# Edits to the schedule of a two-layer convolution and MLP kernel: when transforms, stores, inverses, products and statistics are issued

## The chip, the cores and the metric

The kernel runs on one core of a Trainium2 chip. A core has a matrix engine (TensorE, "PE" in the profile), a vector engine (VectorE, "DVE"), an activation engine (ScalarE, "ACT"), a general one (GpSimd, "POOL") and SyncE ("SP"), which here issues every transfer. Each engine runs its own queue in order and waits on semaphores. The metric is device time in microseconds (us), the median of several executions: 2731.35 us before (2731.3 to 2731.46, three runs).

## The reference: what is computed

Two layers, each an operator A and then an operator B, on 2048 tokens of 1024 channels, all in float32:

```python
def A(x, k, v, shift_k, ssm_k, ssm_D):
    k_shift = causal_conv4(k, shift_k)              # four taps per channel
    kv = k_shift * v
    y = irfft(rfft(kv, 2 * S) * rfft(ssm_k, 2 * S))[:S]   # long causal conv per channel
    return x * (y + kv * ssm_D)

def B(x, w1, b1, w2, b2):
    return relu(x @ w1 + b1) ** 2 @ w2 + b2         # 1024 -> 3584 -> 1024

x = q
x = x + A(layernorm(x), k, v, shift_k, ssm_k, ssm_D)
x = x + B(layernorm(x), w1, b1, w2, b2)
x = x + A(layernorm(x), k, v, shift_k, ssm_k, ssm_D)
x = x + B(layernorm(x), w1, b1, w2, b2)
```

Both layers use the same k, v and filter, so the convolution's result y is computed once and read twice.

## The kernel before, in words

**Units.** The tokens are cut into four blocks of 512. The matrix work is eight units, one for a layer and a block, in the order (layer, block) = (0,0), (1,0), (0,1), (0,2), (1,1), (0,3), (1,2), (1,3). A unit is a row of steps; a step is one piece of weights, mostly 12 matmuls of 512 columns ("the main stream"). A float32 product is made of three matmuls on operands split into a high and a low part (`mm3`, lines 335 to 337). The split of a weight costs a copy on ScalarE (line 1012) and a subtraction on VectorE, at some steps on GpSimd (line 1020); some weights are stored split and loaded back (`wd_m`, line 1010). Between the first and the second unit the block is the same, so the second begins without a break: the last 28 steps of the first unit and the first of the second are made for half the tokens each (6 matmuls a step, later 12 of 256 columns), and the layer norm of each half (`chain`, line 1632) runs meanwhile. The last three units use a scheme with fewer products (`WINO`).

**Convolution.** It runs beside the units, for blocks 1 to 3 (the first block is done ahead of the first unit). Two streams, ticked `FWD_RATE` times a step, transform the inputs channel group by channel group (eight groups of 128 a block):

- `fwd_x` (line 353): loads k and v, four taps and the product with v on VectorE (lines 365 and 367), after some ticks the transposes on TensorE (line 420), the transform (391), sums on VectorE (402 to 407), stores to `xd` (412).
- `fwd_g` (line 429): loads the filter and a carried spectrum `kd`, the transform on TensorE (454), the copy of the new spectrum (459), its store for the next block (463), VectorE's sums (464 to 484), stores to `gd` (493). The PSUM banks `pt` of both streams are taken with `hold` and freed with `give`.

For the second block (`sb <= PLAIN`) the transforms are single float32 matmuls, for the later ones `mm3`. `const_split` splits the transform tables once, when the third block begins.

`prod_stream` multiplies the spectra: GpSimd's product (line 525), two ticks later VectorE's reduction (529), after three products of a group the fold and the butterfly on GpSimd (675 to 680), then the inverse on TensorE (595 for the second block), a copy and a store. Its rate is `pace`: the work of some blocks over the steps left for them, less `PACE_SLACK`. It holds what it is owed; a call gives one product at least, or a None when data is missing, and then the forward streams get one tick more.

**Statistics.** In all units but the first, `prep_a` loads the next block's rows into one of two `px` buffers and takes their mean and variance, from step 28. The bias of a unit is loaded into the same two buffers (line 1737) and added by GpSimd (1741, or 1599 in the last three units).

**Queues.** SyncE issues all transfers in program order, weights among them. A store that waits for its data holds back what is behind it.

Of the kernel before, what the change touches and what calls it, by code (L numbers as in the profile page):

```python
# [21 lines left out]
NT = T // P  # L22
NB = S // T
KT = D // P
FT = F // P
FC = 7
NCH = FT // FC
BL = 256
# [16 lines left out]
AHEAD_0 = 4  # L45
BURST = 1.06
FIN = "GGG"
PACE_SLACK = {1: 74, 3: 10}
PACE_TO = {1: 2}
PLAIN = 1  # L50
FILL = (16, 12, 8)
# [14 lines left out]
PIECES = ((0, 0), (0, 1), (1, 0), (1, 1))  # L66
WLO = {"b": "GGGV", "x": "GGGV"}
PREP_PACE = 0.2
FWD_RATE = {0: 1.4, 1: 1.4, 2: 1.4, 3: 1.1, 4: 1.1, 5: 1}


# [169 lines left out]
def tile_h3_mlp(ctx: ExitStack, tc: tile.TileContext, q, kT, vT, shk, ssmT, ssmD, w1, b1, w2, b2,  # L241
# [111 lines left out]
    def fwd_x(sb, c):  # L353
        k4 = mkfx([P, T + 3])
        SY.dma_start(k4, kT[c * P:(c + 1) * P, sb * T:sb * T + T + 3])
        v4 = mkfx([P, T])
        SY.dma_start(v4, vT[c * P:(c + 1) * P, sb * T:(sb + 1) * T])
        for _ in range(FWD_WAIT):
            yield
        ks = mkfx([P, T])  # L360
        w = shkt[:, c]
        A.activation(ks, k4[:, 3:], AF.Copy, scale=w[:, 0:1])
        yield
        for s in range(1, 4):
            V.scalar_tensor_tensor(ks, k4[:, 3 - s:T + 3 - s], w[:, s:s + 1], ks, op0=OP.mult, op1=OP.add)
        yield
        V.tensor_mul(ks, ks, v4)
        for _ in range(4 if sb == 1 else 7):
            yield
        o, = yield from hold(1)  # L370
        transposes(o, ks)
        yield
        if sb <= PLAIN:
            xt = mkfx([P, T])
            A.copy(xt, o)
        else:
            hi = mkfx([P, T], F32R)
            lo = mkfx([P, T], F32R)
            A.copy(hi, o)
            yield  # L380
            V.tensor_sub(lo, o, hi.bitcast(F32))
        yield
        give(o)
        yield
        oa = yield from hold(2)
        for e in range(2):
            for r in range(2):
                q_ = slice(e * 256, e * 256 + 256)
                ou = oa[e][:, r * 256:r * 256 + 256]
                if sb <= PLAIN:  # L390
                    PE.matmul(ou, plain[0][:, 2 * e + r], xt[:, q_], start=True, stop=True)  # L391
                else:
                    mm3(ou, fh[:, 2 * e + r], fl[:, 2 * e + r], hi[:, q_], lo[:, q_], True, True)
        yield
        odd = mkfx([P, T])
        A.copy(odd, oa[1])
        yield
        xo = cv.tile([P, 2, T], F32, name="fy", bufs=1)
        xv = xo.rearrange("p r (n u c) -> p u (r n) c", u=2, c=CG)
        ev = oa[0].rearrange("p (n c) -> p n c", c=CG)  # L400
        ov = odd.rearrange("p (n c) -> p n c", c=CG)
        V.tensor_add(xv[:, 0], ev, ov)
        V.tensor_sub(xv[:, 1], ev, ov)
        yield
        give(*oa)
        x2 = mkfx([P, T])
        V.tensor_add(x2, xo[:, 0], xo[:, 1])
        yield
        yield
        for i in range(3):  # L410
            t = x2 if i == 2 else xo[:, i]
            SY.dma_start(dview(XD[i], sb, c), t.rearrange("p (g b u) -> p g b u", g=2, b=BT))
        yield
# [15 lines left out]
    def fwd_g(sb, c):  # L429
# [28 lines left out]
        for r in range(2):  # L458
            A.copy(kk[r][:, BL:], oa[r])
        yield  # L460
        if sb < NB - 1:
            for r in range(2):
                SY.dma_start(KD[sb][c][:, r], kk[r][:, BT * BL:])
        V.scalar_tensor_tensor(kk[1][:, 0:T], kk[1][:, 0:T], sgn[:, 1:2], oa[0], op0=OP.mult, op1=OP.add)
        V.scalar_tensor_tensor(oa[1], kk[0][:, 0:T], sgn[:, 0:1], oa[1], op0=OP.mult, op1=OP.add)
        yield
# [20 lines left out]
            yield  # L487
            yield
        give(*oa)
        yield  # L490
        yield
        for i in range(3):
            SY.dma_start(dview(GD[i], sb, c), go[i].rearrange("p (g b u) -> p g b u", g=2, b=BT))
        yield
# [4 lines left out]

    def fwd_stream(kind, fwd):  # L500
        for sb in range(1, NB):
            if sb > PLAIN:
                const_split()
            for c in range(KT):
                yield from fwd(sb, c)
                half_done[kind].add((sb, c))
                if all((sb, c) in d for d in half_done.values()):
                    plag.at(3, fwd_done.add, (sb, c))

    streams = [fwd_stream("x", fwd_x), fwd_stream("g", fwd_g)]  # L510

    def fwd_tick():
# [6 lines left out]
    def prod_stream():  # L519
# [11 lines left out]
        def fin(st, sm, sb, g, k):  # L531
# [4 lines left out]
                lag.at(1, fin, st, sm, sb, g, 1)  # L536
            elif k == 1 and sb <= PLAIN:
                st["z"] = butterfly(E, s)
                lag.at(2, fin_plain, st, sb, g, 0)
            elif k == 1:  # L540
                pair = st["pair"]
                if "l" not in pair if g % 2 else inv[1] < inv[0]:
# [1235 lines left out]
    for s, (k, u, c, a, i, tts, w) in enumerate(steps):  # L1778
# [3 lines left out]
        if u != cur_u:  # L1782
            cur_u = u
            if u:
                xT = nxt
            bst = {}
            if u in WINO:
                wacc, rp = {}, {}
# [99 lines left out]
            early.append(load_y(b, HALF[0]))  # L1888
        if u + 1 < NU and not direct[u]:
            n = s - start_step[u]  # L1890
            if n == 28:
                pa = prep_a(*ORDER[u + 1])
            elif n > 28 and pa is not None and next(pa, 0) == 0:
                pa = None
            if u in WINO and left == W_PREP:
                nxt = prep_w(*ORDER[u + 1], lag)
            elif u not in WINO and left == 18:
                while pa is not None:
                    if next(pa, 0) == 0:
                        pa = None  # L1900
                close_conv(ORDER[u + 1][1])
                nxt = prep_b(*ORDER[u + 1], lag)
# [6 lines left out]
                next(tgen[0], None)  # L1909
        busy = left <= 18 and u + 1 < NU  # L1910
        rate = pace.get(u, 100) * (PREP_PACE if busy else 1.0)
        if len(tts) < NT:
            rate *= 0.1
        owed += rate
        todo = min(owed, BURST * rate)
# [64 lines left out]
```

## Time and profile before

| what | value |
|---|---|
| median of three runs | 2731.35 us |
| the profiled execution | 2731.19 us |
| its span in the trace | 2729.4 us |
| TensorE busy | 2683.3 us (98%) |
| VectorE busy | 1989.7 us (73%) |
| GpSimd busy | 843.9 us (31%) |
| DMA, mean | 277 GB/s |

The trace is of one execution. Busy times are shares of the span; a matmul's end is modelled, so TensorE's pace is read from the starts of matmuls that follow each other. "Idle before" names the time for which an engine stood ahead of an instruction, and what released it. The main stream's matmuls are counted from the end of the first block's own part; the first unit's half steps begin at 1272 and the second unit's full steps at 1632.

### The profile page before, as it was taken

The page shows a single profiled execution, that of the slowest core. Times are in us where ns is not written, and L with a number is a line of the kernel's source. Part 1 is how long each engine was busy: PE and PEld are TensorE (multiplying, and loading weights), DVE is VectorE, ACT ScalarE, POOL GpSimd, SP SyncE. Part 2 cuts the span into 40 slices and gives each one's busy share as a digit, 9 for nine tenths or more (in the row PEclk, how much of TensorE's full clock was granted, in tenths as well). Part 3 has the DMA queues.
Part 4 walks back from the last instruction along what each step waited for, and adds up shares of the span by engine and source line. Part 5 has one row for each costly group of instructions (what it writes and reads, how often), then busy time and mean ns, then how long its engine had stood idle before and what let it go on. Part 6 is the DMA issues. An engine that isn't in the chain of part 4 may idle for free.

```text
span 2729.4 us, 36532 instructions
## 1 busy us (share of the span) xinstructions
PE 2683.3 (98%) x12568; PEld 2228.9 (82%) x12568; DVE 1989.7 (73%) x3066; ACT 1124.2 (41%) x1936; POOL 843.9 (31%) x532
## 2 busy tenths in 40 slices
PE   7999999999999999999999999999999999999999
PEld 6888787888888888888888888888788788888887
DVE  7878888788987877779677665366787666664555
ACT  4454344433444233442234422244455444445443
POOL 2336565345532655236543454000100010001000
PEclk9999999999999999999999999999999999999999
DMA  8789898699989898888977887688888866676545
GB/s 253 262 301 316 285 312 285 221 312 369 324 298 324 295 338 280 267 332 284 349 263 269 301 295 253 226 288 311 300 284 295 281 229 211 229 276 200 178 166 204
DMA packets 377482, 755.05 MB, mean 277 GB/s; under 512 B 43840, under 2 KB 159184, under 8 KB 377296
## 3 DMA queue, kind: packets, MB, share of 16 engines
q1 hardware_dynamic: 377296, 752.72, 80.6%
q8 instruction: 99, 1.62, 0.2%
q14 instruction: 87, 0.71, 0.1%
HBM read 602.63 MB, written 149.95 MB: 276 GB/s over the span
## 4 chain that ended last, share of the span: by engine, by line
PE 84%; DVE 6%; DMA 5%; issue 1%; POOL 1%; ACT 1%; SPq 1%; DVEq 0%; ACTq 0%; POOLq 0%
PE p L336 26%; PE p L335 26%; PE p L337 26%; DMA wr<-w 2%; PE p L1095 2%; DVE whl L1020 1%; PE pt L335 1%; PE pt L337 1%; PE pt L336 1%; DMA whl<-wd_m 1%; DVE sm L529 0%; DMA cx<-xd 0%; PE pt L391 0%; DMA cg<-gd 0%; PE p L789 0%
## 5 line engine op out<-in xcount | busy, mean ns | idle before, releaser
L525 POOL TENSOR_TENSOR cp<-cx,cg 128x384 f32<-128x384 f32 (+5 forms) x288 | 541.8, 1893 | 580.3 <-DVE sm L529 388.1
L335 PE MATMUL p<-xh,whl 128*128 128x512 f32 (+1 forms) x1840 | 706.6, 384 | 3.3 <-DMA whl<-wd_m 2.5
L337 PE MATMUL p<-xh,whl 128*128 128x512 f32 (+1 forms) x1840 | 703.6, 382 | 3.6 <-DVE whl L1020 2.8
L336 PE MATMUL p<-xl,whl 128*128 128x512 f32 (+1 forms) x1840 | 702.8, 382 | 0.1
L1012 ACT CAST whl<-wr 128x512 fp32r<-128x512 f32 x637 | 383.5, 619 | 441.6 <-PE p L337 262.4
L1020 DVE TENSOR_TENSOR whl<-wr,whl 128x512 fp32r<-128x512 f32 x622 | 500.4, 825 | 78.4 <-ACT whl L1012 73.2
L335 PE MATMUL p<-whl,rh 128*128 128x512 f32 x1372 | 548.1, 399 | 3.7 <-ACT whl L1012 2.4
L336 PE MATMUL p<-whl,rh 128*128 128x512 f32 x1372 | 543.7, 396 | 1.9 <-POOL whl L1020 1.7
L337 PE MATMUL p<-whl,rl 128*128 128x512 f32 x1372 | 542.6, 396 | 0.0
L337 PEld LDWEIGHTS p<-xh,whl 128*128 128x128 f32 x1840 | 345.9, 188 | 71.7 <-DVE whl L1020 3.0
L335 PEld LDWEIGHTS p<-xh,whl 128*128 128x128 f32 x1840 | 346.2, 188 | 70.5 <-DMA whl<-wd_m 2.6
L336 PEld LDWEIGHTS p<-xl,whl 128*128 128x128 f32 x1840 | 346.0, 188 | 66.1 <-DVE xl L1408 0.3
L335 PEld LDWEIGHTS p<-whl,rh 128*128 128x128 f32 x1372 | 259.5, 189 | 64.0 <-ACT whl L1012 3.9
L336 PEld LDWEIGHTS p<-whl,rh 128*128 128x128 f32 x1372 | 259.5, 189 | 61.9 <-POOL whl L1020 2.6
L337 PEld LDWEIGHTS p<-whl,rl 128*128 128x128 f32 x1372 | 259.4, 189 | 60.6
L1502 DVE TENSOR_TENSOR rl<-wr,rh 128x512 fp32r<-128x512 f32 x140 | 141.1, 1009 | 182.8 <-ACT rh L1497 182.7
L1599 POOL TENSOR_TENSOR acc<-acc,px 128x512 f32<-128x512 f32 x18 | 23.1, 1317 | 771.0 <-DMA px<-b 771.0
L529 DVE TENSOR_REDUCE sm<-cp 128x128 f32<-128x384 f32 (+5 forms) x288 | 249.3, 874 | 9.2 <-POOL cp L525 9.2
L1494 ACT ACTIVATE wr<-p,b1t 128x512 f32<-128x512 f32 x138 | 95.2, 690 | 379.1 <-PE p L337 375.3
L1563 DVE TENSOR_TENSOR rl<-wr,rh 128x256 fp32r<-128x256 f32 x84 | 49.8, 593 | 208.5 <-ACT rh L1558 208.4
L1622 DVE TENSOR_TENSOR acc<-p,acc 128x512 f32<-128x512 f32 x152 | 101.5, 687 | 87.3 <-PE p L337 86.9
L1555 ACT ACTIVATE wr<-p,b1t 128x512 f32<-128x512 f32 x84 | 57.9, 689 | 190.4 <-PE p L337 188.9
(277 smaller groups left out, 3310.9 us busy)
## 6 DMA issues: line engine op xcount, KB each, us to landing
whl<-wd_m SPq DMA_DIRECT2D x379, 512.0 KB, 5.1
wr<-w SPq DMA_DIRECT2D x493, 256.0 KB, 5.4
wr<-td SPq DMA_DIRECT2D x152, 256.0 KB, 4.1
wd_m<-whl SPq DMA_DIRECT2D x70, 512.0 KB, 6.0
cx<-xd SPq DMA_DIRECT2D x48, 512.0 KB, 5.7
cg<-gd SPq DMA_DIRECT2D x48, 512.0 KB, 6.4
gd<-fg SPq DMA_DIRECT2D x72, 256.0 KB, 6.2
cx<-xd SPq DMA_DIRECT2D x48, 384.0 KB, 5.8
```

The source lines that it names most:

```text
L335: PE.matmul(o, lh, rh, start=start, stop=False)
L336: PE.matmul(o, lh, rl, start=False, stop=False)
L337: PE.matmul(o, ll, rh, start=False, stop=stop)
L525: G.tensor_mul(pr.rearrange("p c i -> p i c"), xt[:, 0:j + 1], gt[:, j::-1])
L529: V.tensor_reduce(sm[:, ty, jj], st["pr"], axis=AX.X, op=OP.add)
L1012: A.copy(t[:, 0], raws[n]["t"])
L1020: ENG[e[n % len(e)]].tensor_sub(t[:, 1], raws[n]["t"], t[:, 0].bitcast(F32))
L1095: PE.matmul(o, lh, r, start=start, stop=stop)
L1494: A.activation(r, st["o"], AF.Relu, bias=b1t[:, st["f"]:st["f"] + 1])
L1502: V.tensor_sub(st["lo"], st["r"]["t"], st["hi"].bitcast(F32))
L1555: A.activation(r, st["o"], AF.Relu, bias=b1t[:, st["f"]:st["f"] + 1])
L1622: V.tensor_add(accs[tt][:, d], o, accs[tt][:, d])
```

## The change

Line numbers in this text are those of the kernel before; the new file's differ by up to six, from line 510 to 1785 by four, so that 525 reads 529 and 1020 reads 1024.

- Second block, `fwd_x`: seven ticks instead of four between the product and the transposes.
- `fwd_g`: the carried spectrum is stored behind `give`, no longer ahead of the sums. Two ticks more ahead of the stores to `gd` for the second block.
- The third block's streams wait until the second unit has begun (`second`).
- Second block's inverse: three ticks behind the butterfly, not two.
- Statistics in the sixth and seventh unit from step 45, not 28.
- Products: `PACE_SLACK` 78 for 74; the rate falls to a tenth `QUIET` = 4 steps ahead of the half steps too.

```diff
-PACE_SLACK = {1: 74, 3: 10}
+PACE_SLACK = {1: 78, 3: 10}
...
+QUIET = 4
...
-        for _ in range(4 if sb == 1 else 7):
+        for _ in range(7):
             yield
         o, = yield from hold(1)
         transposes(o, ks)
...
-        if sb < NB - 1:
-            for r in range(2):
-                SY.dma_start(KD[sb][c][:, r], kk[r][:, BT * BL:])
         V.scalar_tensor_tensor(kk[1][:, 0:T], kk[1][:, 0:T], sgn[:, 1:2], oa[0], op0=OP.mult, op1=OP.add)
...
         give(*oa)
-        yield
-        yield
+        if sb < NB - 1:
+            for r in range(2):
+                SY.dma_start(KD[sb][c][:, r], kk[r][:, BT * BL:])
+        for _ in range(4 if sb <= PLAIN else 2):
+            yield
         for i in range(3):
             SY.dma_start(dview(GD[i], sb, c), go[i].rearrange("p (g b u) -> p g b u", g=2, b=BT))
...
         for sb in range(1, NB):
+            while sb > PLAIN and not second:
+                yield
             if sb > PLAIN:
                 const_split()
...
+    second = []
...
                 st["z"] = butterfly(E, s)
-                lag.at(2, fin_plain, st, sb, g, 0)
+                lag.at(3, fin_plain, st, sb, g, 0)
...
             if u:
                 xT = nxt
+                second.append(u)
...
             n = s - start_step[u]
-            if n == 28:
+            at = 45 if u in WINO else 28
+            if n == at:
                 pa = prep_a(*ORDER[u + 1])
-            elif n > 28 and pa is not None and next(pa, 0) == 0:
+            elif n > at and pa is not None and next(pa, 0) == 0:
                 pa = None
...
-        if len(tts) < NT:
+        if len(tts) < NT or direct[u] and left < 4 * FC + QUIET:
             rate *= 0.1
```

What the order of instructions shows of it, at three places. First, SyncE's queue at the fourth channel group of the second block (`kd_3` is its carried spectrum, `wd_m` stored weights, `wr` raw weights, `cx` and `cg` operands of the products, `gd` the filter's spectra). Before, and then of the change:

```order
L463 DMA kd_3_88<-fk 128x256 x2
L1001 DMA wr<-w 128x512
L1004 DMA wr<-w 128x512
L1028 DMA wd_m_1_5_0_2445<-whl 128x1024
L1004 DMA wr<-w 128x512 x5
L625 DMA cx<-xd_73 128x512
L625 DMA cg<-gd_74 128x512
L1004 DMA wr<-w 128x512
L1028 DMA wd_m_1_6_0_2523<-whl 128x1024
L493 DMA gd_74<-fg 128x2x256
```

```order
L490 DMA kd_3_88<-fk 128x256 x2
L1008 DMA wr<-w 128x512
L1032 DMA wd_m_1_0_2_2609<-whl 128x1024
L1008 DMA wr<-w 128x512 x2
L629 DMA cx<-xd_71 128x512
L629 DMA cg<-gd_75 128x512
L629 DMA cx<-xd_72 128x512
L629 DMA cg<-gd_76 128x512
L494 DMA gd_74<-fg 128x2x256
```

The carried spectrum's store has moved towards that of `gd`, and other loads stand between them. Second, SyncE's queue where the first unit's half steps begin, before and then of the change (`yd` is the convolution's result, `fg` the filter's load for the third block, `xd` the input's spectra):

```order
L1004 DMA wr<-w 128x512
L606 DMA yd_102<-wr 512x1x64
L625 DMA cx<-xd_73 128x512
L625 DMA cg<-gd_74 128x512
L625 DMA cx<-xd_71 128x512
L625 DMA cg<-gd_75 128x512
L427 DMA fg<-ssmT 128x2x128 x2
L436 DMA fk<-kd_1_86 128x256 x2
L606 DMA yd_102<-wr 512x1x64
L1028 DMA wd_m_3_0_0_4506<-whl 128x1024
L1004 DMA wr<-w 128x512 x3
```

```order
L1008 DMA wr<-w 128x512 x7
L413 DMA xd_71<-fy 128x2x256
L413 DMA xd_72<-fy 128x2x256
L413 DMA xd_73<-fx 128x2x256
L629 DMA cx<-xd_72 128x512
L629 DMA cg<-gd_76 128x512
L1032 DMA wd_m_3_0_0_4363<-whl 128x1024
L1008 DMA wr<-w 128x512 x4
L1032 DMA wd_m_3_0_2_4401<-whl 128x1024
L1008 DMA wr<-w 128x512
L629 DMA cx<-xd_73 128x512
L629 DMA cg<-gd_74 128x512
```

The third block's loads are gone, seven weight loads stand together, and operand loads of products follow within the half steps (four more stand behind the last row). Third, GpSimd's queue where the second unit begins, before and then of the change (line 1741, now 1745, adds the bias; 1020, now 1024, splits a weight; 525, now 529, is a product):

```order
L1020 TENSOR_TENSOR whl<-wr,whl 128x512
L1741 TENSOR_TENSOR acc<-acc,px 128x1024 x4
L1020 TENSOR_TENSOR whl<-wr,whl 128x512
L525 TENSOR_TENSOR cp<-cx,cg 128x4x128
L1020 TENSOR_TENSOR whl<-wr,whl 128x512
L525 TENSOR_TENSOR cp<-cx,cg 128x3x128
L525 TENSOR_TENSOR cp<-cx,cg 128x4x128
```

```order
L1024 TENSOR_TENSOR whl<-wr,whl 128x512 x8
L1745 TENSOR_TENSOR acc<-acc,px 128x1024 x4
L529 TENSOR_TENSOR cp<-cx,cg 128x3x128
L529 TENSOR_TENSOR cp<-cx,cg 128x4x128
L1024 TENSOR_TENSOR whl<-wr,whl 128x512
L529 TENSOR_TENSOR cp<-cx,cg 128x3x128
L529 TENSOR_TENSOR cp<-cx,cg 128x4x128
L529 TENSOR_TENSOR cp<-cx,cg 128x3x128
L529 TENSOR_TENSOR cp<-cx,cg 128x4x128
L1024 TENSOR_TENSOR whl<-wr,whl 128x512
```

Two products stand between the bias and the next weight split now, where there was none, and four ahead of the one after it.

## Rows read from the trace of the kernel before

**Rows 1.** The page's part 1: engine, busy us, share, instructions.

```profile
PE 2683.3 (98%) x12568; PEld 2228.9 (82%) x12568; DVE 1989.7 (73%) x3066; ACT 1124.2 (41%) x1936; POOL 843.9 (31%) x532
```

**Rows 2.** Waits of TensorE from 200 to 2729 us: in total, times, longest.

```profile
PE pt L420 <- DVE fx L367: 6.9, 3, 6.0
PE p L335 <- DMA whl<-wd_m: 3.6, 4, 2.2
PE p L337 <- DVE whl L1020: 2.8, 1, 2.8
PE p L335 <- ACT whl L1012: 2.4, 2, 1.9
PE pt L595 <- DVE fg L484: 2.0, 1, 2.0
```

**Rows 3.** Timeline of TensorE, 285 to 310: start, us, instruction, idle before.

```profile
293.35 0.39 PE L337 MATMUL p<-whl,rl 128*128 128x512 f32 x1
293.58 1.05 PE L595 MATMUL pt<-sm,yh 128*128 128x128 f32 x8
300.66 1.10 PE L420 MATMUL pt<-ident,fx 128*128 128x128 f32 x4 [6.03 <-DVE fx L367]
...
304.97 0.63 PE L337 MATMUL p<-whl,rl 128*128 128x512 f32 x1
305.40 0.63 PE L335 MATMUL p<-whl,rh 128*128 128x512 f32 x1
```

**Rows 4.** Windows: us, busy PE, PEld, DVE, ACT, POOL, clock, DMA share, GB/s.

```profile
460.00:480.00 20.00, 17.90 (x69) 13.90 (x69) 10.10 (x16) 6.62 (x11) 2.32 (x2) 0.91 1.00 362
...
520.00:540.00 20.00, 20.00 (x171) 20.00 (x171) 12.17 (x14) 11.34 (x19) 9.11 (x6) 1.00 0.45 157
...
620.00:640.00 20.00, 20.00 (x98) 16.87 (x97) 19.86 (x25) 9.99 (x17) 15.28 (x9) 1.00 1.00 321
```

**Rows 5.** Timeline of VectorE, 282 to 302.

```profile
292.29 3.68 DVE L365 SCALAR_TENSOR_TENSOR fx<-fx,shkt 128x512 f32<-128x512 f32 x3
...
299.84 0.68 DVE L367 TENSOR_TENSOR fx<-fx 128x512 f32<-128x512 f32 x1
```

**Rows 6.** Waits of SyncE, 250 to 302.

```profile
SPq L493 <- DVE fg L484: 9.9, 2, 5.5
```

**Rows 7.** Waits of SyncE, 440 to 470.

```profile
SPq L493 <- DVE fg L484: 8.8, 1, 8.8
```

**Rows 8.** Timeline of TensorE, 440 to 480.

```profile
465.83 0.49 PE L335 MATMUL p<-whl,rh 128*128 128x512 f32 x1 [1.87 <-ACT whl L1012]
466.55 0.76 PE L336 MATMUL p<-whl,rh 128*128 128x512 f32 x1 [0.23 <-DVE whl L1020]
...
469.67 0.57 PE L337 MATMUL p<-whl,rl 128*128 128x512 f32 x1
```

**Rows 9.** Timeline of VectorE, 476 to 548.

```profile
522.21 1.00 DVE L1701 TENSOR_SCALAR wr<-acc,mv,rs 128x512 f32<-128x512 f32 x2
...
539.94 5.70 DVE L1502 TENSOR_TENSOR rl<-wr,rh 128x512 fp32r<-128x512 f32 x2
```

**Rows 10.** Timeline of GpSimd, 495 to 548.

```profile
534.24 10.85 POOL L1741 TENSOR_TENSOR acc<-acc,px 128x1024 f32<-128x1024 f32 x4
545.05 1.71 POOL L1020 TENSOR_TENSOR whl<-wr,whl 128x512 fp32r<-128x512 f32 x1
```

**Rows 11.** Timeline of TensorE, 480 to 560: two stretches.

```profile
518.77 0.39 PE L337 MATMUL p<-xh,whl 128*128 128x256 f32 x1 [2.78 <-DVE whl L1020]
...
526.57 1.04 PE L1710 MATMUL p<-ident,wr 128*128 128x128 f32 x8
...
546.82 0.39 PE L337 MATMUL p<-xh,whl 128*128 128x256 f32 x1 [0.81 <-POOL whl L1020]
```

**Rows 12.** Groups of GpSimd by line and shape: busy us, mean ns, idle before.

```profile
L525 POOL TENSOR_TENSOR cp<-cx,cg 128x512 f32<-128x512 f32 x48 | 71.5, 1490 | 15.4 <-DVE sm L529 15.4
```

**Rows 13.** Waits of SyncE, 1895 to 1942.

```profile
SPq L725 <- POOL fk L1599: 8.9, 1, 8.9
```

## The prediction

> **What bounds the kernel now.** Read the page's first part first: TensorE is busy for 2683.3 of 2729.4 us [rows 1]. Nearly all of it is work that the change neither adds nor takes away, so what can move is the 46 us of idle time, and time at the lower clock. What the first block loses comes ahead of everything the diff touches. Second, what TensorE waits for behind 200 us: 6.9 us for the second block's transposes, which want VectorE's product of line 367 (6.0 in one piece), 2.0 for an inverse behind line 484, 2.4 and 2.8 for weights split late, 3.6 for stored weights of which 2.2 in one piece [rows 2]. Third, the timeline around the longest. TensorE stands from 294.6 to 300.66; then twelve matmuls follow each other 0.43 us apart instead of 0.23, the pitch just before (304.97 to 305.40 against 293.35 to 293.58) [rows 3]: the 1.2 GHz level in place of 2.4. Twelve times 0.2, with the slower transposes, is 2.3 us more. So this place costs 8.3.
>
> Why was the product late? VectorE was never idle ahead of it. Three shifted multiplies from 292.29 took 3.68 us, and only at 299.84, behind adds and weight splits, came line 367 with 0.68 [rows 5]; the product itself is short, VectorE was behind. SyncE's queue suffers from the same lag: the filter spectrum's store (line 493) waited for line 484 for 9.9 us in two pieces [rows 6], and again for 8.8 us [rows 7]. Every load behind it waits too, which is where the weight that is late at 465.83 comes from [rows 8]. One lag of VectorE thus makes the waits at 294, 446 and 465 us.
>
> **The change part by part.** Counting main-stream matmuls in the order of instructions (12 are one step, 12 x 0.23 = 2.76 us), the second block's transposes stood 12 to 36 behind line 367 and stand 36 to 48 behind it now; the late one had 24. That is 2.8 us more slack. The store of line 493 moves from 12 to 36 matmuls behind the last line-484 add to 36 to 48. The store of the carried spectrum moves from at most 12 behind its copy to 48 or 60; its reader comes a whole block later, so I cost that at nothing. A channel now takes 132 matmuls instead of 122 (180 to 1104 against 180 to 1032 for seven), so VectorE has 8% less to do per step: over the roughly 300 matmuls (69 us) ahead of the late transposes, at a VectorE near full, 5.5 us. Together 8.3 us against a wait of 6.0, so it goes, with its clock loss: -8.3. The two smaller waits of the kind go: -0.9. What is late next is a split weight or an inverse of the same size; I leave +0.6 for it, bounds 0 and 6.0.
>
> The third block's first spectrum, which ran ahead of 1248 matmuls, is out of the first unit; the inverse behind its line 484 loses that wait: -2.0 (bounds 0 and -2.0). At 465.83 and 466.55 the wait is 1.87 and 0.23, and eight matmuls to 469.67 stand at the lower pitch, 1.6 [rows 8]: 3.7 in all (the window's clock of 0.91 says 1.8 for the last part [rows 4]). With the store no longer blocking and seven weight loads issued ahead of the halves this goes as well: -3.7.
>
> Against that, **the pause does not empty this stretch**. The rate falls to a tenth, but a stream with work owed still gives one product per step, and its start is later now: five products fall into the first half-steps where one did, and six loads of product operands (256 KB each) stand together in SyncE's queue ahead of a weight. The last two need the buffer of the product just issued, so SyncE waits for GpSimd there. Bounds 0 and 3.7 (the wait that stood here); I take 1.0, near the lower end, since eight half-steps of 1.38 us lie between that weight's load and its use.
>
> In the last half's layer norm, the constants' split (768 columns, about 1.0 us at the rate of the 0.68 us row), and ahead of its last normalisation three line-365 multiplies, 2.0 us at 0.68 [rows 5], 3.7 beside GpSimd, are new on VectorE. What lies beside them: the second norm ended near 523.2 [rows 9] for transposes at 526.57 [rows 11], some 3 us of cover. The split is not covered, since the weight wait at 518.77 [rows 11] follows this chain; a reduce that leaves takes some of it back. I take +0.9, bounds 0 and 4.7 (all four, with the slow multiplies).
>
> **The start of the second unit** is where I expect the change to cost most. GpSimd adds the bias from 534.24 for 10.85 us; the weight split behind it started at 545.05 [rows 10] and TensorE waited 0.81 us for it [rows 11]. Now two products stand between, 1.49 us each [rows 12]: the split comes 3.0 us later. Two inverses moved ahead (0.9 more TensorE work by then) hide less than one; +3.0, bounds 0 and 8.3 (the longest wait with its clock).
>
> Beside these four adds two of VectorE's two-input operations of this width (0.68 us in [rows 5]) took 5.70 us [rows 9]. The Trainium skill, page "SBUF — State Buffer", section "Who interferes with whom", says that a VectorE instruction with two SBUF inputs and a GpSimd instruction that reads SBUF shut each other out for a whole instruction; the trace agrees with these rows, and by that rule the twelve products now issued between 1560 and 1680 matmuls speak against the change. What that would make of the time is the first rival.
>
> Second unit: the third block's products run from 1824 to 2304 matmuls for what had 1752 to 2280, 10% denser, and all its eight channels fall here. VectorE was already busy 19.86 of 20 us from 620 to 640, though TensorE kept its 20.00 there [rows 4]. +1.5, bounds 0 and 8.3. The pace constant (74 to 78) lies inside this: the products end at the same step.
>
> Statistics: in the sixth unit SyncE waited 8.9 us to load the next row block into a buffer that GpSimd's bias add held [rows 13], and stored weights came 2.2 us late, the longest of their four [rows 2]. The loads now stand behind the add, at step 45: -2.2. VectorE's own wait for the first row block stays as it was.
>
> Sum: -8.3 -0.9 -2.0 -3.7 -2.2 = -17.1; +0.6 +1.0 +0.9 +3.0 +1.5 = +7.0; together -10.1. The profiled execution took 2731.19 us (its span and 1.8 around it), 0.16 under the median of 2731.35; against the median, 2721.2.
>
> On the clock: 2.78 us of waiting at 518.77 [rows 11] was followed by the upper level (1.00 from 520 to 540), 1.87 at 465.83 by the lower (0.91 from 460 to 480) [rows 4]. The Trainium skill, page "TensorE: Matmul & The Clock Gate", section "Part 1: The HAM clock gate", says that idling brings the half rate and activity lifts it again; by that alone the new 3.8 us wait would cost about 2.3 more, 2723.5. Rows stand on both sides here, so the sum has none of it and the range has it.
>
> **Rivals.** (1) VectorE chained to GpSimd at the second unit's start. Each reduce there stands on VectorE ahead of a weight split and waits for a product that itself queues behind the 10.85 us of adds. For it: the rows above. Against it: weights are split three or more steps ahead, 8.3 us. Price: 3.0 becomes 8.3 with the clock, and another 1.5: 2728. (2) The pause doesn't do what it says, and the wait at the halves stays whole: 1.0 becomes 3.7, 2724. For it: five products and six loads in the order. Against: seven weights loaded first. (3) Slower: the lag only moves to the second unit. From 1824 matmuls on VectorE has more to do than the steps last; once it is more than the 8.3 us lead behind, each further us is TensorE's, and the store of line 493 there (12 to 36 matmuls behind its add, not moved for this block) blocks SyncE again, as it did twice in the first unit. Two such waits of 8.3 less the 1.5 already in the sum: 2721.2 + 15.1 = 2736.3, and with what stays of the first unit's, 2738. Against it: a full stretch there cost TensorE nothing before [rows 4], and 1680 to 1824 has fewer products than before.
>
> **How the numbers follow.** Chances: forecast 0.58, its own range 2714 to 2726; (1) 0.18, (2) 0.13, (3) 0.11. 0.2% is 5.5 us, about what a measurement of this kernel tells from no change: faster is under 2725.9, slower over 2736.8. Nearly all of the forecast and of (2) and a quarter of (1) are faster: 0.71; most of (1) and a third of (3) are the same: 0.21; the rest of (3) slower: 0.08. The range is 2713 (every gain, -17.1, and a little) to 2733, which leaves out most of (3).
>
> **What would show it.** Right: no wait of transposes for line 367 over 1 us and no clock under 1.00 around 300; SyncE's waits of line 493 under 4 us; no wait near 465; none for stored weights in the sixth unit; a wait of 3 to 4 us for GpSimd's split at the second unit's start. Wrong: a wait over 5 us anywhere from 440 to 720, a granted clock under 0.95 in the second unit, or a wait of the same size for line 367 at another channel.

## The result and the profile after

The changed kernel took 2742.34 us (median of six runs, 2738.1 to 2747.44) against 2731.32 us for the kernel before in runs beside it: ratio 1.0041, 95% interval 1.0027 to 1.0056. It is slower by 0.41%; the forecast was 2721.2 us with a range of 2713 to 2733. The profiled execution took 2740.9 us, its span is 2739.1 us, 9.7 more than before.

The page's first part: busy time and share of each engine. TensorE was busy for 2690.1 of 2739.1 us, so it idled 49.0 us in place of 46.1 [rows 1]; the mean granted clock fell from 0.998 to 0.996.

```profile
PE 2690.1 (98%) x12568; PEld 2231.4 (81%) x12568; DVE 1973.6 (72%) x3066; ACT 1123.1 (41%) x1936; POOL 841.0 (31%) x532
```

Waits of TensorE from 200 us to the end: what for, us in total, times, longest. They answer to [rows 2].

```profile
PE p L336 <- DMA whl<-wd_m: 6.9, 9, 2.0
PE p L336 <- ACT whl L1016: 5.3, 1, 5.3
PE p L338 <- DVE whl L1024: 3.3, 1, 3.3
PE pt L337 <- DVE yl L565: 2.4, 2, 1.7
PE pt L336 <- DVE fy L404: 2.4, 1, 2.4
PE p L338 <- POOL whl L1024: 1.7, 1, 1.7
```

The 6.9 us for line 367 are gone, whole, and so is the inverse's wait. In their place stand 5.3 us in one piece for a weight split, twice as much for stored weights, and sums and inverses of the third block that VectorE brings late. Where they lie is seen in windows (busy time of TensorE, weight loads, VectorE, ScalarE, GpSimd, then granted clock, DMA share, GB/s). The kernel before, four long stretches:

```profile
200.00:440.00 240.00, 233.15 (x1074) 193.97 (x1073) 209.22 (x298) 101.11 (x186) 147.99 (x119) 0.99 0.92 304
440.00:500.00 60.00, 53.50 (x232) 41.94 (x231) 47.99 (x87) 25.77 (x45) 20.18 (x15) 0.97 0.78 270
560.00:1000.00 440.00, 439.44 (x2074) 366.04 (x2073) 365.31 (x511) 171.00 (x308) 209.95 (x127) 1.00 0.94 326
1900.00:2720.00 820.00, 815.61 (x3571) 664.68 (x3571) 534.45 (x967) 384.23 (x632) 31.06 (x24) 1.00 0.71 240
```

The changed kernel, the same four, and three short ones in which the clock fell:

```profile
200.00:440.00 240.00, 240.00 (x1112) 199.82 (x1111) 203.86 (x295) 103.28 (x187) 142.81 (x116) 1.00 0.92 306
440.00:500.00 60.00, 53.73 (x267) 44.57 (x266) 47.31 (x91) 24.33 (x42) 16.51 (x13) 0.94 0.80 274
560.00:1000.00 440.00, 431.98 (x2031) 358.60 (x2030) 364.79 (x506) 170.31 (x307) 208.38 (x126) 1.00 0.93 324
1900.00:2720.00 820.00, 815.58 (x3562) 662.01 (x3560) 527.46 (x959) 385.64 (x636) 30.58 (x24) 1.00 0.70 237
...
460.00:480.00 20.00, 14.15 (x49) 10.70 (x48) 14.87 (x36) 5.57 (x10) 2.55 (x2) 0.83 0.62 220
500.00:520.00 20.00, 16.73 (x130) 16.53 (x129) 13.55 (x28) 7.68 (x14) 2.16 (x2) 0.91 0.32 118
740.00:760.00 20.00, 16.05 (x75) 13.29 (x74) 14.45 (x19) 6.39 (x12) 14.15 (x10) 0.91 0.91 309
```

From here on "loss" is TensorE's idle time plus, in 20 us windows, their length times what the granted clock lacks of 1 (idle time at a lower clock is in both). So counted, the change gave 10.5 us back from 200 to 440 us, and lost 1.4 more from 440 to 500, 3.9 from 500 to 540, 3.6 from 540 to 600, 8.5 from 600 to 1000 and 0.8 up to 1900; from 1900 on nothing moved (4.4 before and after). Together, with 0.3 won ahead of 200 us, a net loss of 7.4 of the 9.7 us; the rest is below what these windows resolve.

**The half steps.** Where the 5.3 us come from is read on three queues. On ScalarE the copy of the awaited weight (1016) stands behind the layer norm's activations (1685), and those wait for VectorE:

```profile
468.61 1.48 ACT L1685 ACTIVATE p<-acc,nm,rs 128x512 f32<-128x512 f32 x2 [1.28 <-DVE nm L1653]
471.50 1.49 ACT L1685 ACTIVATE p<-acc,nm,rs 128x512 f32<-128x512 f32 x2 [1.41 <-DVE acc L1663]
472.93 0.60 ACT L1016 CAST whl<-wr 128x512 fp32r<-128x512 f32 x1
```

The raw weight itself was not late. By the semaphore that the copy waits for, it is the second of two loads that SyncE issued from 451.70 on, and it had landed by 459.5. What was late is the layer norm. VectorE stood 3.8 us for the split of the weight before, whose copy ScalarE began only at 462.76, when by the profile TensorE was done with a buffer; the layer norm's first add (1670) stands behind that split:

```profile
451.70 1.19 SPq L1008 DMA_DIRECT2D wr<-w  x2
...
462.76 0.62 ACT L1016 CAST whl<-wr 128x512 fp32r<-128x512 f32 x1 [3.85 <-PE p L338]
...
463.42 0.69 DVE L1024 TENSOR_TENSOR whl<-wr,whl 128x512 fp32r<-128x512 f32 x1 [3.77 <-ACT whl L1016]
464.03 0.68 DVE L1670 TENSOR_TENSOR acc<-p,acc 128x512 f32<-128x512 f32 x1
```

SyncE stood for 5.3 us too, from 457.3 on, ahead of a load of a stored weight, until a store had landed:

```profile
SPq L1014 <- DMA wd_m<-whl: 5.3, 1, 5.3
```

This is not what TensorE waits for here, though it is as long: the raw weight that SyncE asked for behind it (463.09) landed at 466.77 and is copied only after 479 us.

TensorE goes on at 473.58, at the lower pitch (0.43 between starts, 476.38 to 476.81; the 1.2 GHz level as in [rows 3]):

```profile
473.58 0.79 PE L336 MATMUL p<-whl,rh 128*128 128x512 f32 x1 [5.29 <-ACT whl L1016]
...
476.38 0.63 PE L337 MATMUL p<-whl,rh 128*128 128x512 f32 x1
476.81 0.63 PE L338 MATMUL p<-whl,rl 128*128 128x512 f32 x1
```

**The second unit's start.** GpSimd: the bias add (1745), two products (529), and the weight split that TensorE waited 1.7 us for. The forecast had this wait at 3 to 4 us, from 3.0 us of products [rows 10, 12]; they took 2.29:

```profile
520.37 10.84 POOL L1745 TENSOR_TENSOR acc<-acc,px 128x1024 f32<-128x1024 f32 x4
531.16 2.29 POOL L529 TENSOR_TENSOR cp<-cx,cg 128x384 f32<-128x384 f32 x2
533.40 1.71 POOL L1024 TENSOR_TENSOR whl<-wr,whl 128x512 fp32r<-128x512 f32 x1
```

What the forecast did not have here is SyncE: an operand load's buffer comes free only with those products, so SyncE stood for 7.6 us behind GpSimd, and the stored weight behind it left at 538.75 and cost TensorE 2.0 us and a stretch of low clock (540 to 560 us: 0.91):

```profile
529.28 0.44 SPq L629 DMA_DIRECT2D cg<-gd  x1
537.38 0.32 SPq L629 DMA_DIRECT2D cx<-xd  x1
...
538.75 0.38 SPq L1014 DMA_DIRECT2D whl<-wd_m  x1
```

SyncE's waits for products from 440 to 540 us (in total, times, longest), and TensorE's for that weight:

```profile
SPq L629 <- POOL cp L529: 8.9, 3, 7.6
```

```profile
544.66 0.64 PE L336 MATMUL p<-whl,rh 128*128 128x512 f32 x1 [2.04 <-DMA whl<-wd_m]
```

### The profile page after: what moved, and what is told of

Read it like the earlier page. It is cut to its first block, busy times and chain, and to the rows that moved or that the text cites. A ratio compares the mean times of both kernels' runs of the same rounds, so it can differ in the third digit from the quotient of the medians.

```text
span 2739.1 us, 36524 instructions
## 1 busy us (share of the span) xinstructions
PE 2690.1 (98%) x12568; PEld 2231.4 (81%) x12568; DVE 1973.6 (72%) x3066; ACT 1123.1 (41%) x1936; POOL 841.0 (31%) x532
## 4 chain that ended last, share of the span: by engine, by line
PE 84%; DMA 6%; DVE 5%; issue 2%; POOL 1%; ACT 1%; SPq 0%; DVEq 0%; ACTq 0%; POOLq 0%
PE p L337 26%; PE p L336 26%; PE p L338 26%; PE p L1099 2%; DMA whl<-wd_m 1%; DMA wd_m<-whl 1%; DVE whl L1024 1%; PE pt L337 1%; PE pt L338 1%; PE pt L336 1%; POOL acc L1745 1%; PE pt L392 1%; PE pt L455 1%; PE p L793 1%; DMA cg<-gd 0%
```

## The experiments

Beside each: the median, the ratio to the kernel before run on the same chip, and the 95% interval. The loss by stretch is that of each run's one profiled execution. Executions of the kernel before spread from 2728.3 to 2739.5 us, so a few us in a single row say little; the ratios, and what several rows share, say more:

| run | ratio | 200 to 440 us | 440 to 540 | 540 to 1400 |
|---|---|---|---|---|
| before | | 10.5 | 11.1 | 1.5 |
| changed | 1.0041 | 0.0 | 16.4 | 14.0 |
| e1 no gate | 1.0056 | 0.0 | 20.9 | 17.5 |
| e2 no pause | 1.0059 | 0.0 | 16.0 | 17.4 |
| e3 delays alone | 1.0055 | 0.0 | 16.5 | 23.3 |
| e4 gate alone | 1.0008 | 10.1 | 8.4 | 10.4 |
| e5 delays, rate 1.6 | 1.0030 | 11.9 | 13.7 | 3.7 |
| e6 rate 1.32 alone | 1.0055 | 1.1 | 18.0 | 20.3 |
| e7 carried store alone | 1.0012 | 11.2 | 13.4 | 0.6 |
| e8 changed, rate 1.6 | 1.0076 | 10.1 | 9.2 | 16.4 |
| e9 eight loads left out | 1.0019 | 0.0 | 10.9 | 13.6 |
| e10 half the operands | 1.0014 | 0.9 | 16.7 | 13.6 |
| e11 short reduces | 1.0025 | 0.0 | 18.7 | 11.4 |
| e12 statistics alone | 1.0003 | 10.5 | 11.3 | 0.9 |
| e13 every 4th split | 1.0014 | 8.5 | 12.7 | 0.7 |
| e14 every 8th split | 1.0012 | 11.8 | 10.5 | 1.2 |
| e15 slow, then fast | 1.0032 | 11.4 | 9.0 | 8.1 |
| e16 e10 and e11 | 0.9991 | 0.0 | 16.3 | 2.5 |

**e1 to e4: which part does it?**

e1, the changed kernel without the gate:

```diff
-            while sb > PLAIN and not second:
-                yield
```

> The changed kernel, but the third block's transforms start in the first unit again, as before; all else stays changed. Theory 1 (moving that work into the second unit is what takes the gain back: SyncE's queue, the DMA engines and VectorE are too full there): the waits at 504 to 513, 540 to 560, 640 to 660 and 740 to 760 us, which are 14 us worse than in the kernel before, go; about 2728 us, ratio to before 0.999, between 2724 and 2732. Theory 2 (the products that are paused and then stand ahead of the halves do it): the gate is beside the point, 2738 to 2743, with the 5.3 us wait near 468 us still there. Theory 3 (the longer delays of the second block make products late): also 2738 to 2743.

2749.96 us, 1.0043 to 1.0069. Theory 1 fell as an account of the whole: without the gate the kernel is no faster, and the losses behind 500 us stay. e2, without the pause:

```diff
-        if len(tts) < NT or direct[u] and left < 4 * FC + QUIET:
+        if len(tts) < NT:
```

> The changed kernel without the pause of products in the last steps ahead of the halves; the products ahead of the halves are issued at the full rate. Theory 2: the wait of 5.3 us near 468 us with its low clock goes back to at most the 3.7 us that it was before or vanishes: 5 to 9 us faster than the changed kernel, ratio to before about 1.001 to 1.002. Theory 1: the wait at the halves may change by some us but the 14 us that were lost behind 500 us stay: ratio 1.002 to 1.005. If the pause is of use: slower than the changed kernel, over 1.005.

2750.75 us, 1.0046 to 1.0071. Theory 2 fell too: the wait of 5.3 us in one piece is gone, but smaller ones stand in its place (2.4, 1.9 and 1.1 us, and the last half's 3.3), and the loss from 440 to 540 us is the same. The pause is of some use or of none; the intervals of e2 and of the changed kernel overlap. e3, the delays on the kernel before (all four edits of the second block, with the carried store's move):

```diff
-        for _ in range(4 if sb == 1 else 7):
+        for _ in range(7):
...
-        yield
-        yield
+        for _ in range(4 if sb <= PLAIN else 2):
+            yield
...
-                lag.at(2, fin_plain, st, sb, g, 0)
+                lag.at(3, fin_plain, st, sb, g, 0)
```

> The kernel before with the second block's delays alone: transposes 7 ticks behind their product, the carried spectrum's store behind the release of its tiles, 4 ticks ahead of the filter spectrum's store, the plain inverse one step later. Third block, pause, pace and statistics as before. Theories 1 and 2: the 6.0 us wait with its low clock at 294 to 305 us goes (8.3 in all), with the two small ones, and little else moves: 2721 to 2724 us, ratio 0.9965 to 0.9975. Theory 3: products come later and stand in the half steps, so a wait of 5 us or more comes up near 465 us: ratio 0.998 to 1.001.

2749.42 us, 1.004 to 1.0069: beyond what any theory had. The delays, which the forecast booked as the gain of 8.3 + 0.9, bring that gain whole and lose 27 us behind it. e4, the gate on the kernel before:

```diff
+            while sb > PLAIN and not second:
+                yield
             if sb > PLAIN:
```

> The kernel before with one edit: the third block's transforms don't start before the second unit. Theory 1: the second unit loses as it does in the changed kernel, 14 us behind 500 us, less 2 us for an inverse that no longer waits in the first unit and some of the 6 us wait at 294 us if the first unit is less full: 2737 to 2744, ratio 1.002 to 1.005. Theories 2 and 3: no loss of that size, 2727 to 2732, ratio 0.9985 to 1.000.

2735.7 us, 1.0 to 1.0017: at most a small loss. It mends 440 to 500 us (2.4 lost, for 8.3) and pays for it in the second unit, which loses 10.4 us where the kernel before lost 1.5: in that stretch theory 1 was right. The larger loss is the delays', so they were the place to look.

**e5 to e8: the delay, or the longer channel?** A delay does two things: its instruction stands further behind its data, and the channel takes longer. The rate `FWD_RATE` of the first unit sets the second apart. In the order of instructions the third block's spectra start at 1704 and 1872 main-stream matmuls before, at 1764 and 1944 in e3, at 1692 and 1848 in e5, at 1776 and 1956 in e6. The edit of e5 (on e3) and of e8 (on the changed kernel); in e6 (on the kernel before) the first number is 1.32:

```diff
-FWD_RATE = {0: 1.4, 1: 1.4, 2: 1.4, 3: 1.1, 4: 1.1, 5: 1}
+FWD_RATE = {0: 1.6, 1: 1.4, 2: 1.4, 3: 1.1, 4: 1.1, 5: 1}
```

> The second block's four delays on the kernel before, as in the run of the delays alone, but with the rate at which its transforms advance in the first unit raised from 1.4 to 1.6 per step: a channel takes 132 matmuls in the middle of the unit as without the delays, and the third block's spectra start at 1692 and 1848 matmuls as in the kernel before (1704, 1872) and not at 1764 and 1944. Theory C (the delays cost by stretching a channel, which sets everything behind it later and denser): the loss of 27 us behind 440 us goes, the wait at 294 us stays away: 2720 to 2727 us, ratio 0.996 to 0.998. Theory D (the later stores and transposes themselves cost: loads and products wait for them): still 1.003 to 1.006.

> The kernel before without any of the changes, but with that rate lowered from 1.4 to 1.32: a channel is stretched as the delays stretch it and the third block's spectra start at 1776 and 1956 matmuls. Theory C: the loss behind 440 us comes as with the delays, 15 to 27 us, less what the wait at 294 us may give back as VectorE has less to do per step: 2736 to 2758 us, ratio 1.002 to 1.010. Theory D: nothing of that size, ratio 0.998 to 1.001.

e6, with none of the change's edits: 2748.91 us, 1.0043 to 1.0068, the ratio of e3, with gain and loss of e3 in the table. Waits of TensorE in e6, 200 to 440 us:

```profile
PE pt L420 <- DVE fx L367: 1.1, 1, 1.1
```

and from 540 to 1000 us:

```profile
PE pt L336 <- DVE yl L561: 4.7, 2, 4.4
PE p L335 <- DMA whl<-wd_m: 4.0, 3, 2.2
```

e5: 2741.17 us, 1.0019 to 1.0041. With the delays but short channels the second unit keeps its time (3.7) and the first loses as before: the transposes are not late any more, other work of VectorE is. Its longest waits from 200 to 440 us:

```profile
PE p L336 <- DVE whl L1020: 2.7, 1, 2.7
PE pt L391 <- ACT wr L601: 2.2, 1, 2.2
PE pt L595 <- DVE fg L481: 2.1, 1, 2.1
```

The longer channel alone makes the gain and the loss of e3; the slack of the delays gained nothing by itself (e5's channels are a little shorter than those of the kernel before, so its VectorE has slightly more to do per step). e8:

> The changed kernel with that rate raised from 1.4 to 1.6: every part of the change, but the second block's channels as short as before. Theory C: the loss of the delays goes and that of the gate stays (about 4 us by the run of the gate alone): 2722 to 2732 us, ratio 0.9965 to 1.0. Theory D: as the changed kernel, 1.003 to 1.006.

2753.49 us, 1.0062 to 1.009: theory C expected a gain and was wrong here. The half steps are better for it (4.0 from 440 to 500 us, for 9.7), but the first unit is late again (10.1) and the second stays crowded (16.4): with short channels the gate is enough for that, as with long ones it takes no gate (e1, 17.5). e7, the carried store alone:

```diff
-        if sb < NB - 1:
-            for r in range(2):
-                SY.dma_start(KD[sb][c][:, r], ...)     # ahead of the sums
...
         give(*oa)
+        if sb < NB - 1: ...                            # the same store
```

> The kernel before with one edit: the carried spectrum's store stands behind the release of the two tiles, just ahead of the filter spectrum's stores. No instruction of TensorE, VectorE or GpSimd moves. Theory C and D: 0.999 to 1.001. Theory K (five stores together fill the DMA queues and make weights late): 1.002 to 1.006.

2737.55 us, 1.0003 to 1.0021: between the theories, a small loss.

**e9: the halves.**

```diff
+            if 3 * NG - 8 <= n < 3 * NG - 4:
+                got[n] = got[3 * NG - 9]
+                when[n] = lag.n
+                return
```

> The changed kernel, but eight of the 256 KB operand loads that it issues between 1224 and 1296 matmuls, just ahead of the half steps and in them, are left out: those products read the operands loaded before, so part of the second block's convolution is computed from the wrong data. The products stay, at the same places. Theory L (these loads stand ahead of weights in SyncE's queue and on the DMA engines, so the weight of the 5.3 us wait near 468 us is late): that wait and its low clock go, the loss from 440 to 500 us (9.7 us of idle time and low clock) falls to 3 us or less; 6 to 8 us less than the changed kernel, ratio to before 1.001 to 1.002. Theory N (ScalarE splits that weight behind the layer norm's activations, which wait for VectorE; the loads are beside the point): the wait stays over 4 us, ratio 1.003 to 1.005.

2737.36 us, 1.0011 to 1.0028, some 6 us under the changed kernel, give or take 5, by the profile as well (span 2735.6 against 2739.1). At the place of the 5.3 us (line numbers are four higher there: 1020 is the copy, 1674 the layer norm's first add):

```profile
457.84 0.62 ACT L1020 CAST whl<-wr 128x512 fp32r<-128x512 f32 x1 [1.90 <-DMA wd_m<-whl]
...
459.39 0.69 DVE L1674 TENSOR_TENSOR acc<-p,acc 128x512 f32<-128x512 f32 x1 [0.20 <-PE p L338]
...
468.31 0.60 ACT L1020 CAST whl<-wr 128x512 fp32r<-128x512 f32 x1
...
468.96 0.50 PE L336 MATMUL p<-whl,rh 128*128 128x512 f32 x1 [0.51 <-ACT whl L1020]
```

Without the loads the wait is 0.5 us: theory L holds in that they bring it about. Theory N holds for the way it takes: the awaited copy stands right behind the activations here as well, and it is early because the copy of the weight before came 4.9 us earlier (457.84 for 462.76) and the layer norm with it 4.6 us (459.39 for 464.03). Why the loads hold that first copy is not settled: in the changed kernel it waits for TensorE to be done with a buffer, here for a store to land, so the two programs may have given it different buffers. And such loads are not enough by themselves: in e8 four of them stand as far ahead of the same copies (455.71 to 458.44), SyncE stood 5.1 us for a store, and TensorE waited 2.1 us. From 440 to 540 us e9 lost 10.9 us for 16.4. Of the 6.6 us up to 500, 3.3 are the wait of the last half's layer norm, which the changed kernel has behind 500 us.

**e10, e11, e16: the second unit.**

```diff
+                got[n][1] = got[n][0]        # third block: cg not loaded (e10, e16)
...
+                    st["pr"] = st["pr"][:, :, :2]   # third block's reduces (e11, e16)
```

> The changed kernel, but the third block's products read one operand twice, so the load of the other operand, half of the bytes of these loads in the second unit, is left out (that part of the convolution is then wrong). The products, reduces and all else stay. Theory M (in the second unit the DMA engines, busy 1.00 from 600 to 720 us, bound it: stored weights and tables come late): the loss of 13.5 us of idle time and low clock from 540 to 1000 us falls under 4: ratio to before 0.999 to 1.001. Theory V (VectorE, busy 54 of 60 us there, is late): as the changed kernel, 1.003 to 1.005.

> The changed kernel, but the third block's reduces on VectorE add up two elements in place of 5 to 8 per sum (that part of the convolution is then wrong): each takes some 0.3 us in place of 0.8. Loads and products stay. Theory V: VectorE has 0.5 us less to do per product, the waits for it behind 540 us go and what hangs on them: 5 to 10 us less than the changed kernel, ratio to before 1.000 to 1.002. Theory M: as the changed kernel, 1.003 to 1.005.

> The changed kernel with both of the third block's reliefs: one operand's loads left out and the reduces cut to two elements (that part of the convolution is then wrong). If VectorE and the DMA engines together make the second unit late, the loss from 540 to 1000 us (13.5 us in the changed kernel) falls under 3 us: ratio 0.9985 to 1.000. If it stays over 6 us, it is the order itself (SyncE's queue behind GpSimd and behind stores just issued), ratio 1.001 to 1.003.

e10: 2736.79 us, 1.0006 to 1.0023; e11: 2739.63 us, 1.0015 to 1.0034; e16: 2730.54 us, 0.9982 to 1.0001. Against the changed kernel's 1.0041, less for the DMA engines is worth about 7 us, less for VectorE about 4, both together 14, each give or take 5: the first and the last are clear of noise, the second is not, and the shares roughly add up. (e10's profile is of its slowest run, so its row in the table is high.) The stretch 540 to 1000 us before and changed, then in e10, e11 and e16, one each:

```profile
540.00:1000.00 460.00, 458.63 (x2197) 383.36 (x2196) 382.83 (x528) 183.59 (x329) 226.74 (x137) 1.00 0.93 321
540.00:1000.00 460.00, 449.95 (x2107) 373.10 (x2106) 379.23 (x531) 176.74 (x319) 224.01 (x140) 0.99 0.92 321
```

```profile
540.00:1000.00 460.00, 452.09 (x2116) 375.40 (x2115) 377.89 (x532) 177.91 (x321) 225.60 (x142) 0.99 0.85 286
```

```profile
540.00:1000.00 460.00, 450.94 (x2119) 373.89 (x2118) 335.65 (x533) 178.85 (x323) 226.31 (x142) 1.00 0.93 322
```

```profile
540.00:1000.00 460.00, 458.04 (x2170) 381.55 (x2169) 349.10 (x547) 178.85 (x322) 230.15 (x144) 1.00 0.87 292
```

TensorE idles 1.4 us before, 10.1 changed, then 7.9, 9.1 and 2.0. Neither VectorE nor the DMA engines alone make this stretch late. In e10 most of the waits that are left are for VectorE (3.8 us for the inverse's input, 2.1 for the sums), in e11 most are for stored weights (4.9). A chain in the changed kernel shows how they meet (start, us, what ended last):

```profile
729.51 5.94 DMA whl<-wd_m
...
735.46 8.65 DMA fg<-ssmT
...
756.18 0.61 DVE fy L404
```

The filter's load takes 8.65 us among the others, VectorE gets the work that needs it late, and the transform's sums (404) come 2.4 us late for TensorE.

**e12: the statistics.**

```diff
+            at = 45 if u in WINO else 28
-            if n == 28:
+            if n == at:
```

> The kernel before with one edit: the statistics of the Winograd units start at step 45 and not at 28. As the prediction had it, the 2.2 us wait for a stored weight near 1925 us goes: 2728.5 to 2730 us, ratio 0.999 to 0.9995. Rival: the stored weights are late there for another reason, or the wait comes up elsewhere in the unit: 0.9995 to 1.001.

2733.94 us, 0.9995 to 1.0012: no gain. SyncE's 8.9 us behind GpSimd [rows 13] are gone, but TensorE's waits from 1900 to 2180 us (before: 3.0 for stored weights, 0.7 for line 1606) are these:

```profile
PE p L335 <- DMA whl<-wd_m: 2.1, 2, 1.2
PE p L336 <- DVE whl L1020: 1.0, 2, 0.6
```

**e13 to e15: is the first unit's gain to be had without the loss?**

```diff
+WLO = {"b": "GGGV", "x": "GGGV", "0": "VVVG"}   # e13; e14: "VVVVVVVG"
...
+        fowed += (FWD_RATE.get(u, 2) if u else 1.3 if s < 65 else 1.6) * ...   # e15
```

> The kernel before, with every fourth weight split of the first unit's full steps on GpSimd in place of VectorE; no channel is stretched and nothing behind moves in the order. VectorE has some 3.7 us less to do per 60 us (5.4 splits of 0.68). Theory C (the price is the moved work): the wait for line 367 near 294 us goes or halves and nothing is lost behind 540 us: 2721 to 2729 us, ratio 0.996 to 0.999. Rival (GpSimd, busy 42 of 60 us, takes 1.3 to 1.7 us for each such split and products come late for it): waits for GpSimd's splits, ratio 1.000 to 1.004.

> The same with every eighth split: VectorE has 1.8 us less per 60 us. Theory C: half of the gain of the run with every fourth, ratio 0.997 to 0.9995. Rival: between that run and the kernel before, 1.000 to 1.002.

> The kernel before, with the second block's transforms at 1.3 per step for the first 65 steps and at 1.6 behind, in place of 1.4: channels are stretched only up to the late transposes near 294 us, and the last ends at 1188 matmuls as before (1212), so the third block stays where it was. Theory C: the wait at 294 us shrinks to under 2 us as with the slower rate alone, and nothing is lost in the second unit; VectorE may be late once between 320 and 440 us: 2723 to 2731 us, ratio 0.9965 to 1.000. Rival (VectorE's lag only moves behind 320 us): the same size of wait there, 0.999 to 1.003.

e13: 2737.86 us, 1.0006 to 1.0023; e14: 2735.97 us, 1.0003 to 1.0021; e15: 2742.37 us, 1.0019 to 1.0044. None gains. In e13 the wait for line 367 near 294 us still has 5.0 us in one piece. In e15 it moved behind 320 us, as the rival had it; its waits from 320 to 440 us:

```profile
PE pt L420 <- DVE fx L367: 7.2, 2, 4.2
```

No kernel tried here that computes the whole result beats the kernel before.

## Why the prediction was wrong, step by step

- **What bounds it, and the 294 us stall.** Right: VectorE's lag made it, and it went. -8.3 - 0.9 + 0.6 was forecast for 200 to 440 us, -10.5 came: the whole loss of this stretch (its share of clock is counted as 3.6 here, as 2.3 there). VectorE was not quite "never idle" ahead of the stall: it stood 1.14 us at 286.91 for a product. Of the two reasons given, 5.5 us of less work per step was the right one (e6 has it alone); the 2.8 us of more slack was not (e5 has it, and the lag shows up at weight splits).
- **The step that failed: the second unit's crowding, +1.5.** "A channel now takes 132 matmuls instead of 122" was booked as a gain of 5.5 us, and the third block's start behind the first unit as a gain of 2.0; what both push into the second unit stood in the sum as +1.5, with bounds 0 to 8.3. It measured 9.2 (560 to 1000 us: 8.0 idle and 1.8 of low clock, against 0.6). VectorE's 8% less per step in the first unit is work of the third block that comes 60 to 84 matmuls later (e3, e6). Either push alone makes such a loss: the longer channel (e6 20.3 us from 540 to 1400, e1 17.5) and the gate (e4 10.4, e8 with short channels 16.4), against 1.5 before and 14.0 with both. e16 puts it on VectorE and the DMA engines together. The reason against it, that "a full stretch there cost TensorE nothing before", held for the order before only. Rival 3 had the mechanism ("the lag only moves to the second unit"), at 0.11; its store of line 493 blocking SyncE is not what came (5.5 us in four waits from 540 to 1400): SyncE's long waits there, other than for TensorE, are for GpSimd's products (41.0 us), for the statistics (17.3) and for stores just issued.
- **The half steps**, -2.0 - 3.7 + 1.0, came as +1.4 (440 to 500 us): -4.7 forecast, 6.1 off. The inverse's wait went, as forecast. The late weight did not: a failed step too. The "seven weight loads issued ahead of the halves" did not help, for the weight was there and the layer norm ahead of its copy was late; eight operand loads bring that about (e9). That they stand there because the second block's last filter spectrum is stored later (411.78 us, before 405.09) is argued, not shown; e8, with short channels (409.37), lost 4.0 us from 440 to 500. Rival 2 was right in kind, that the wait stays; its 3.7 was 5.3 and more low clock.
- **The last half's layer norm**, +0.9: the wait for the weight split behind it grew from 2.8 [rows 11] to 3.3 us, and the clock fell to 0.91 (1.8 us) where it had not before: 2.3, inside the bounds.
- **The second unit's start**, +3.0: from 520 to 560 us 4.7 more, inside the bounds, but in two waits (1.7 for the split, 2.0 for a weight held up in SyncE's queue) and a low clock. VectorE chained to GpSimd (rival 1) does show (3.29 us ahead of a reduce at 532.23), but TensorE's waits are for GpSimd's split and for SyncE's weight.
- **Statistics**, -2.2: 0. The wait of SyncE went; TensorE's was not made by it alone (e12).
- **Together** these terms are off by 17.2 us, of which the second unit is 7.7 and the half steps 6.1: a gain of 10.1 was forecast, a loss of 7.4 is seen in the windows.
- **The clock.** The sum had no loss of the kind behind the first unit. The changed kernel's 20 us windows from 440 us on lack 8.8 us of clock, against 1.8 before: the waits of 5.3, 3.3, 2.0 and 2.4 us (near 468, 500, 544 and 756) were each followed by the lower level, the 2.8 before was not [rows 4, 11]. The rule of the Trainium skill, page "TensorE: Matmul & The Clock Gate", section "Part 1: The HAM clock gate", that idling brings the half rate, agrees with four of these five.

Not settled: how the 9.2 us divide over the two pushes, and over single transfers and sums of the second unit. e1, e3 and e6 lose at different places there (from 540 up to 1340 us), though e3 and e6 have the third block's spectra within 12 matmuls of each other. That the stretch loses almost nothing once both VectorE and the DMA engines have less to do is shown (e16); which transfer is late in a given run is not.

## What to carry to other kernels

A wait that goes because an engine is given less to do per step can be paid where the work is put: before booking the gain, look at the busy time of that engine, and of the DMA engines, in the stretch that receives it (here 83% and 0.94 before anything was moved), and price the move there, not only at the place that is relieved. The shares warn, they do not give the price: they were the same with the loss as without it. To tell a delay's two effects apart (more slack, longer loop), change the loop's rate alone and the delay at the old rate; two runs settle it. Where one queue issues all transfers in order, a load that waits for a buffer can make the weight behind it late (here 7.6 us of SyncE, and 2.0 of TensorE). Two waits of one length near each other need not be one chain: follow the awaited instruction's own input back, queue by queue, before naming the cause.

## What had not been expected of the hardware

In the changed kernel the DMA share from 560 to 1000 us is 0.93 and VectorE is busy 365 of 440 us; the kernel before has 0.94 and 365 and lost 0.6 us there, not 9.8. The same shares thus go with either. That it is decided by when the work comes is inferred, not shown; what is shown is that only both reliefs at once (e16) took the loss away.
